# Values of a sliding-window attention kept in planes of token residues, and loaded in 16 DMAs of 1 MB instead of 128 of 128 KB

## The chip, the core and the metric

The kernel runs on one core of a Trainium2 chip. The metric is the device time of one execution in microseconds (us). The kernel before took 205.69, 203.16 and 200.42 us in three runs; the median is 203.16 us. The profile that is read here is of one execution that took 202.74 us, of which 201.0 us are the span that the profile covers; the other 1.74 us lie around it.

## What is computed

```python
x = A_x                                   # 1 x 2048 x 512, bf16
xn = _layernorm(x)
s = _A_ref(xn, A_wqkv, A_wo)              # attention
g = _silu(_B_ref(xn, B_w1, B_w2, B_w3, B_w4))
return x + s * g

# _A_ref: H = 32 heads of Dh = 16, window W = 8, dilation 2
idx = pos[:, None] - (arange(W) * 2)[None, :]      # token t looks at t, t-2, ..., t-14
logits = einsum("bhsd,bhswd->bhsw", q, kg) * scale # kg, vg: k and v gathered by idx
logits = where(idx >= 0, logits, -1e9)
o = einsum("bhsw,bhswd->bhsd", softmax(logits), vg)
return o @ wo

# _B_ref: a token-shift mixer and an MLP, both with a residual
h = _gelu(_layernorm(x) @ w1)             # quarters of h shifted by +1, -1, +2, -2 tokens
x1 = x + shifted(h) @ w2
return x1 + _gelu(_layernorm(x1) @ w3) @ w4       # w3 512 x 1376, w4 1376 x 512
```

## The kernel before

The 2048 tokens are 16 tiles of 128 tokens and four chunks of four tiles. Nothing is planned at run time: the string ORDER lists about 800 named steps, and the program issues them in that order, so each engine and each DMA queue works through its own steps in the order of that string. A name is a step and a tile (or a chunk and a part): h8 is the step h of tile 8, qk1.3 is part 3 of chunk 1. The steps that the text speaks of:

- st, rsa, rsb, rsc, xn: the first layer norm of a tile (statistics on VectorE, the power -0.5 on GpSimd, the normalized tile on VectorE for chunk 0 and on ScalarE after). tr, xe turn chunk 0 and 1 over on TensorE; tx (line 339) turns the tiles of chunks 2 and 3 over by DMA. xc2 and xc3 load the inputs of those chunks, w3.n and w4.n the MLP's weights.
- h, v, qk: the products with w1, wv and wqk, four matmuls each; he, ve, qe evict them on ScalarE. hst (line 426) turns h over by DMA. vst (line 416) stores a tile of v, 128 tokens x 1 KB, from one of three buffers to the DRAM scratch v_dram, on GpSimd's DMA queue.
- pw, lg: q times k shifted by 2u tokens on VectorE, and the sum over a head's 16 numbers on TensorE, for u = 0 to 7. mask, mx, ls, ex, to, sh, et, ae: the softmax of a chunk and its turn into the tile att. The mask of chunk 0 is seven memsets of -1e9 (line 464).
- lv (line 655): the values of one tile, loaded back from the scratch. A partition of the tile vs holds the pair (u mod 4, token mod 32); along it lie four blocks of 32 tokens and the two halves of u. Each u is a DMA of its own with 128 rows of 1 KB, so a tile takes eight DMAs in two halves (lv5.0 and lv5.1 are u = 0 to 3 and 4 to 7 of tile 5). vs has three buffers.
- pr (line 661): vs times att in place on VectorE. ws (line 670): the sum over u by eight matmuls with the 0/1 matrix sel. oe evicts the sum, oTe (line 690) turns it over by DMA, for the last three tiles on TensorE (ot). wo multiplies by wo, sg and fa multiply by the gate and add x, out stores.
- mix (line 553), xo, s3, xm, x1T (line 586): the mixer of a tile, its layer norm and its turn by DMA. w3c.n and ge: one of the eleven parts of the first MLP product of chunk c and its gelu; w4, yy, si: the second product of a tile and the gate. pl and pr_ copy a few columns of h between neighbouring chunks on GpSimd.

SyncE's queue (SP) issues all loads but two, all DMA transposes and the output stores, each waiting in turn for what it needs.

Of the kernel before, what the change touches and what calls it, by code (L numbers as in the profile page):

```python
# [9 lines left out]
ALU = mybir.AluOpType  # L10
# [7 lines left out]
xn2 rsa3 tr1 xn3 tr2 xe1 xe2 tr3 r2a0 h1 xe3 r2q0 h2 r2b0 he0 h3 v0 he2 hst0 qk0.6 ve0 st6 he1 qk0.0 vst0 w3.1  # L18
st7 qe0.6 pl0 hst1 v2 qe0.0 st4 qk0.3 ve2 st5 hst2 vst2 he3 rsa1.0 qe0.3 rsb1.0 lv0.0 v1 qk0.5 ve1 rsc1.0 r2a1
xn6 qk0.2 vst1 hst3 qe0.5 r2b1 qk0.1 xn4 xc3 qe0.2 mix1 lv0.1 qe0.1 qk0.7 xn5 xo1 xn7 qk0.4 s31 xc2 qe0.7  # L20
tr1.0 qe0.4 lv1.0 tr1.1 xe1.0 mix0 qa1 pw0.0 h4 xe1.1 lv1.1 v5 he4 xo0 qk1.2 st12 ve5 qk1.7 vst5 s30 hst4
qe1.2 st11 lg0.0 qe1.7 qk1.0 lv2.0 pl1 st8 h7 qe1.0 st10 qk1.4 w4.1 he7 st9 qk1.5 lv2.1 pw0.2 qe1.4 pr_0 h5
qe1.5 rsa2.0 st14 rsb2.0 qk1.6 he5 hst7 st15 v3 qe1.6 rsc2.0 hst5 st13 xn8 mix2 r2a2 ve3 v4 tx8 rsa3.0 xn10
r2b2 pw0.1 mix3 xn9 tx10 xo2 rsb3.0 ve4 v7 xo3 xn11 qk1.1 vst4 s32 tx9 ve7 vst3 rsc3.0 qk1.3 r2a3 qe1.1 vst7
w3.0 s33 xn15 lg0.2 r2b3 tx11 lg0.1 pw0.7 qe1.3 h6 xn12 mix4 ra30 he6 pw0.5 rb30 xn13 h8 hst6 xo4 xn14 v8 rc30
s34 he8 v6 xm2 hst8 h10 ve8 ve6 vst8 tx12 lg0.7 xm0 lg0.5 vst6 pw0.4 v10 he10 pl2 x1T0 xm3 h9 pw0.6 ve10 pr_1
tx13 h11 he9 vst10 lg0.6 he11 lg0.4 tx15 mix5 pw0.3 mix7 x1T2 pw1.0 qa2 v11 tx14 xo7 qk2.7 ve11 xo5 w3.3 qk2.1
vst11 s37 qe2.7 w3.2 v13 s35 qe2.1 hst10 xm1 qk2.3 ve13 x1T3 lg0.3 qe2.3 qk2.2 vst13 mask x1T1 qk2.4 pw1.1
qe2.2 v9 hst11 qe2.4 mx0 mix6 ve9 hst9 ls0 v12 vst9 h14 w4.2 xo6 ve12 ex0 s36 qk2.5 vst12 h12 ra31 rb31 v14
he14 to0 w4.0 lg1.0 h15 rc31 sh0 w30.7 qe2.5 he12 qk2.0 ve14 hst12 he15 pw1.2 w30.4 vst14 ge0.7 pl3 hst14 et0  # L30
qe2.0 pr_3 w30.5 ge0.4 ae0 xm5 hst15 w30.9 pr0 ge0.5 w30.1 xm4 pr_2 ge0.9 qk2.6 x1T4 ge0.1 pr1 xm7 ws0 x1T5
lg1.2 qe2.6 lg1.1 w30.10 oe0 lv3.0 pw1.5 v15 ge0.10 w30.8 pw1.3 ve15 x1T7 w30.3 vst15 ge0.8 pr2 xm6 lg1.3
lg1.5 lv3.1 ge0.3 w30.2 w30.6 ge0.2 pw1.4 x1T6 w30.0 ge0.6 pw1.7 ws2 ge0.0 oTe0 lg1.4 oe2 ws1 pw1.6 lg1.7 w42
lv4.0 pw2.4 qa3 pr3 oTe2 qk3.6 oe1 oTe1 w41 qe3.6 yy2 lv4.1 si2 ws3 yy1 lg1.6 w40 oe3 lv5.0 mx1 si1 pw2.0 oTe3
ls1 mix9 lv5.1 qk3.5 xo9 ex1 yy0 mix10 s39 mix8 lv6.0 xo10 qk3.7 qe3.5 xo8 si0 to1 qk3.4 lv6.1 w31.2 s38 qe3.7
w43 qe3.4 sh1 ge1.2 s310 qk3.1 yy3 et1 qe3.1 w31.8 ae1 si3 w31.6 pr4 w31.4 ge1.8 w31.10 pr5 wo.3 mix11 wo.2
ge1.10 w31.9 ge1.4 ge1.6 w31.7 xo11 ge1.9 wo.1 pr6 ws5 ge1.7 lg2.0 oe5 ws4 lg2.4 oe4 lv7.0 w31.3 pw2.1 wo1
ge1.3 pw2.3 wo0 lv7.1 w31.5 sg1 s311 w31.1 ge1.5 oTe5 fa1 wo2 ra32 ge1.1 sg0 rb32 lv8.0 lg2.3 sg2 lg2.1 w31.0
pw2.6 qk3.0 ge1.0 out1 rc32 pw2.5 oTe4 xm8 h13 qe3.0 pr7 w45 xm11 x1T8 he13 xm9 lv8.1 fa0 wo3 fa2 yy5 lg2.5
x1T9 sg3 si5 lg2.6 qk3.3 pw2.2 hst13 w47 pw2.7 qe3.3 xm10 x1T11 fa3 lg2.2 out3 yy7 lg2.7 out2 ws7 out0 mx2 si7  # L40
ws6 x1T10 qk3.2 oe7 oe6 ls2 w44 oTe7 qe3.2 pw3.2 ex2 oTe6 pw3.0 w46 lv9.0 yy4 to2 si4 lv9.1 mix12 yy6 w32.5
sh2 si6 mix14 lv10.0 ge2.5 w32.8 xo12 xo14 et2 ge2.8 lv10.1 w32.1 s312 ae2 w32.10 ge2.1 s314 mix15 ge2.10 pr8
w32.6 mix13 ge2.6 w32.7 xo15 xo13 wo6 ge2.7 s315 wo5 s313 w32.0 sg5 lg3.0 ra33 sg6 ge2.0 ws8 rb33 lg3.2 pr10
oe8 lv11.0 w32.2 w32.4 ge2.2 w32.9 oTe8 rc33 ge2.4 pr9 xm12 w32.3 lv11.1 ge2.9 wo7 xm14 pw3.4 wo4 ge2.3 xm13
x1T12 w411 sg7 sg4 x1T14 pw3.5 x1T13 ws10 fa5 yy11 lg3.5 oe10 lg3.4 w48 pr11 si11 out5 oTe10 xm15 pw3.7 w49
x1T15 yy8 pw3.1 si8 lg3.7 fa4 ws9 pw3.6 out4 lg3.1 oe9 w410 lv12.0 fa7 pw3.3 oTe9 yy9 lg3.6 yy10 lg3.3 si9
ws11 lv12.1 mx3 w33.0 si10 oe11 wo8 fa6 ge3.0 ls3 oTe11 wo10 sg8 w33.2 ex3 lv13.0 sg10 w33.10 fa8 fa10 w33.4
out8 ge3.2 w33.7 to3 out10 lv13.1 w33.5 sh3 ge3.7 w33.8 ge3.10 out6 w33.6 ge3.4 lv14.0 ge3.8 w33.9 ge3.5 ge3.6
et3 ge3.9 w33.1 out7 ae3 lv14.1 w33.3 pr12 ge3.1 wo11 ge3.3 wo9 sg11 ws12 sg9 w412 oe12 lv15.0 fa11 fa9 pr13
out9 w415 lv15.1 pr14 out11 w414 oTe12 yy15 yy12 si15 ws14 yy14 ws13 si12 pr15 w413 oe14 oe13 si14 ot14 yy13  # L50
wo12 oTe14 si13 ws15 sg12 ot13 oe15 wo14 fa12 oTe13 out12 ot15 sg14 wo13 oTe15 fa14 wo15.0 sg13 out14 wo15.1
sg15.0 fa13 out15.0 sg15.1 out13 out15.1
# [4 lines left out]
def kernel(  # L57
# [35 lines left out]
    NB = P // T32  # L93

# [26 lines left out]
    oTp = pool("oTp", 4)  # L121
# [5 lines left out]
    v_dram = dram.tile([PADK + S, D], BF16, name="v_dram")  # L127
# [43 lines left out]
    sel = const.tile([P, T32], BF16, name="sel")  # L171

# [4 lines left out]
    nc.gpsimd.dma_start(out=v_dram[0:PADK, :], in_=zrows[0:PADK, :])  # L177
# [82 lines left out]
    def plan_ln1(c, t, dk):  # L260
# [63 lines left out]
        def tr1(i):  # L324
            if i == 0:
                ps["tr0"] = ps_lg.tile([P, 2, 2, ND, P], BF16, name="tr0_ps", tag="lg")
            pt = ps["tr0"][:, i % 2, i // 2, :, :]
            for dt in range(ND):
                nc.tensor.transpose(pt[:, dt, :], xn_t[i][:, dt * P : (dt + 1) * P], ident[:])

        def xe1(i):
            if i == 0:
                xnT_t[0] = xnTp.tile([P, ND, CH], BF16, name="xnT", tag="xnT")
            nc.scalar.activation(xnT_t[0][:, :, i * P : (i + 1) * P], ps["tr0"][:, i % 2, i // 2, :, :], AF.Copy)  # L334
# [43 lines left out]
    def plan_qkv(c, keys):  # L378
# [36 lines left out]
        def v_s(i):  # L415
            nc.gpsimd.dma_start(out=v_dram[PADK + i * P : PADK + (i + 1) * P, :], in_=vc_t.pop(i))  # L416
# [28 lines left out]
    def plan_logits(c, t, dk):  # L445
# [16 lines left out]
        def mask():  # L462
            for u in range(W - 1):
                nc.vector.memset(lg_t[c][0:32, u, 0 : PADK - DIL * u], -1e9)
# [36 lines left out]
        def turn():  # L501
            pt = ps[f"et{c}"] = mm_tile("et_ps", (P, NB, 2, P), BF16)
            E_n = E_t.pop(c)
            for b in range(NB):
                for uh in range(2):
                    nc.tensor.transpose(  # L506
                        pt[:, b, uh, :],
                        E_n[:, b, U4 * uh : U4 * uh + U4, :].rearrange("p u t -> p (u t)"), ident[:])

        def at_e():  # L510
            at_t[c] = attp.tile([P, NB * 2, TPC, H], BF16, name="att", tag="att")
            nc.vector.tensor_copy(
                out=at_t[c].rearrange("p n j h -> p n (j h)"),
                in_=ps.pop(f"et{c}").rearrange("p b u q -> p (b u) q"))
# [131 lines left out]
    def plan_attend(i, t, tw):  # L646
        c, jj = i // TPC, i % TPC

        def load_vs(uh):
            if uh == 0:  # L650
                vs_t[i] = vsp.tile([P, NB, 2, D], BF16, name="vs", tag="vs")
            vs = vs_t[i]
            for u in range(U4 * uh, U4 * uh + U4):
                r0 = i * P + DIL * u
                nc.sync.dma_start(
                    out=vs[T32 * (u % U4) : T32 * (u % U4) + T32, :, u // U4, :],
                    in_=v_dram[r0 : r0 + P, :].rearrange("(b t) d -> t b d", t=T32))

        def prod():
            vv = vs_t[i].rearrange("p b u (dh h) -> p (b u) dh h", dh=DH, h=H)  # L660
            nc.vector.tensor_tensor(  # L661
                out=vv, in0=vv,
                in1=at_t[c][:, :, jj, :].unsqueeze(2).to_broadcast([P, NB * 2, DH, H]), op=ALU.mult)

        def gather():
            vs = vs_t.pop(i)
            pt = ps[f"o{i}"] = mm_tile("o_ps")
            for uh in range(2):
                for b in range(NB):
# [14 lines left out]
        def ot_e():  # L684
            oT_t[i] = oTp.tile([P, ND, P], BF16, name="oT", tag="oT")
            nc.scalar.activation(oT_t[i], ps.pop(f"ot{i}"), AF.Copy)

        def od():
            oT_t[i] = oTp.tile([P, ND, P], BF16, name="oT", tag="oT")
# [110 lines left out]
```

## Time and profile before

| | us | where |
|---|---|---|
| profiled execution | 202.74 | span 201.0 and 1.74 around it |
| VectorE busy | 165.6 | 82% of the span |
| ScalarE busy | 132.5 | 66% |
| GpSimd busy | 30.8 | 15% |
| products pr on VectorE | 36.3 | 16 of 2287 ns, 128x4096 bf16 |
| sums ws on TensorE | 9.4 | 128 matmuls |
| value loads lv | 128 issues of 302 / 430 / 2331 ns (least, median, most) on SP | 2.3 / 3.0 / 7.3 us from issue to landing |
| value stores vst | 16 issues of 544 ns (median) on GpSimd | 2.0 / 2.9 / 5.4 us to landing |
| turns hst, tx, x1T, oTe | 53 DMA transposes, some 1.2 us of SP each | 2.5 to 3.5 us to landing (medians) |

The page of a profile gives busy times by engine, the span in 40 slices, the DMA queues, the chain of work that ended last, the costliest groups of instructions by line, and the DMA issues. Further views answer for a stretch of time: busy times by window with the mean busy share of the 16 DMA engines and the rate, the instructions in order of time, and who waited for whom. The DMA share of a window can exceed 1 a little, since a packet's time is put to the stretch in which it began.

### The profile page before, as it was taken

What the parts mean: (1) busy time and instruction counts of PE and PEld (TensorE: products, weight loads), DVE (VectorE), ACT (ScalarE), POOL (GpSimd) and SP (SyncE); (2) the same over time, 40 slices, a digit from 0 to 9 for tenths busy, and PEclk for the clock granted to TensorE, in tenths of its full rate; (3) what the DMA queues carried; (4) which work ended last, traced back from release to release, by engine and by line L of the source; (5) the groups of instructions that cost most, each with busy time, mean ns of one, the idle gap of its engine ahead of it and who ended that gap; (6) DMA issues with size and microseconds to landing.
All of it is one profiled execution on the core that took longest, in us unless ns stands there. A gap on an engine that the chain in (4) does not pass through costs nothing.

```text
span 201.0 us, 3994 instructions
## 1 busy us (share of the span) xinstructions
PE 187.4 (93%) x1470; PEld 90.0 (45%) x1496; DVE 165.6 (82%) x265; ACT 132.5 (66%) x204; POOL 30.8 (15%) x48
## 2 busy tenths in 40 slices
PE   7599999939999999999999999999999999999991
PEld 7344544413444444454444444445444444444440
DVE  5752667993496799997999999899999999689854
ACT  3498856595837799727689639497446629953370
POOL 4015220692731411120000020000020000000000
PEclk9999999996999999999999999999999999999999
DMA  5988999999699654766985446666937567798302
GB/s 186 343 260 188 256 248 256 253 141 243 153 108 258 165 169 95 203 144 179 224 215 139 116 126 181 176 116 172 252 76 203 129 138 186 215 258 248 93 29 79
DMA packets 57908, 36.27 MB, mean 180 GB/s; under 512 B 31794, under 2 KB 56864, under 8 KB 57888
## 3 DMA queue, kind: packets, MB, share of 16 engines
q1 hardware_dynamic: 56416, 33.24, 67.8%
q0 software_dynamic: 800, 2.11, 3.2%
q10 hardware_dynamic: 672, 0.66, 1.0%
q8 instruction: 12, 0.20, 0.4%
q14 instruction: 8, 0.07, 0.2%
HBM read 24.84 MB, written 4.21 MB: 145 GB/s over the span
## 4 chain that ended last, share of the span: by engine, by line
PE 86%; DMA 4%; ACT 4%; DVE 3%; issue 1%; ACTq 0%; DVEq 0%
PE w_ps L608 19%; PE w_ps L623 19%; PE qk_ps L393 13%; PE v_ps L405 7%; PE w_ps L553 6%; PE h_ps L405 6%; PE wo_ps L715 6%; PE lg L457 4%; PE o_ps L670 4%; DMA xnT<-xn 3%; DMA x_all<-in_A_x_dram 1%; DVE stats L262 1%; PE et_ps L506 1%; ACT vct L411 1%; ACT xn L308 1%
## 5 line engine op out<-in xcount | busy, mean ns | idle before, releaser
L448 DVE TENSOR_TENSOR pw<-qT,kT 128x2048 bf16<-128x2048 bf16 x32 | 38.2, 1216 | 5.3 <-PE lg L457 5.1
L608 PE MATMUL w_ps<-x1nT,w_sb 128*128 128x512 bf16 (+1 forms) x168 | 41.1, 380 | 0.4
L623 PE MATMUL w_ps<-w_sb,h3t 128*128 128x512 bf16 (+1 forms) x171 | 39.4, 379 | 0.5 <-issue 0.3
L661 DVE TENSOR_TENSOR vs<-vs,att 128x4096 bf16<-128x4096 bf16 x16 | 36.3, 2287 | 0.2
L615 ACT ACTIVATE h3t<-w_ps 128x512 bf16<-128x512 f32 (+1 forms) x44 | 25.1, 605 | 12.9 <-PE w_ps L608 12.6
L393 PE MATMUL qk_ps<-xnT,wqk_sb 128*128 128x512 bf16 x122 | 30.4, 379 | 0.5 <-issue 0.3
L623 PEld LDWEIGHTS <-h3t 128*128 128x128 bf16 (+1 forms) x176 | 16.7, 98 | 20.7 <-issue 0.8
L608 PEld LDWEIGHTS <-w_sb 128*128 128x128 bf16 (+1 forms) x176 | 16.9, 100 | 19.1 <-DMA vs<-v_dram 0.4
L405 PEld LDWEIGHTS <-xnT 128*128 128x128 bf16 x128 | 12.6, 101 | 16.8 <-issue 2.3
L553 PE MATMUL w_ps<-w_sb,hT 128*128 128x512 bf16 x63 | 16.2, 379 | 3.6 <-DMA hT<-ht 3.6
L393 PEld LDWEIGHTS <-wqk_sb 128*128 128x128 bf16 x128 | 12.2, 98 | 14.9 <-issue 0.4
L676 ACT ACTIVATE o_sb<-o_ps 128x512 bf16<-128x512 f32 x16 | 9.5, 598 | 12.8 <-DMA oT<-o_sb 3.7
L405 PE MATMUL v_ps<-wv_sb,xnT 128*128 128x512 bf16 x62 | 17.2, 398 | 0.1
L405 PE MATMUL h_ps<-w_sb,xnT 128*128 128x512 bf16 x61 | 16.0, 393 | 1.0 <-ACT xnT L334 0.7
L632 ACT ACTIVATE g<-g 128x512 bf16<-128x512 bf16 x16 | 10.0, 629 | 10.1 <-DVE g L629 10.0
L262 DVE BATCH_NORM_STATS2 stats<-x_all 128x6 f32<-128x512 bf16 x16 | 10.8, 675 | 4.7 <-DMA x_all<-in_A_x_dram 4.7
L715 PE MATMUL wo_ps<-wo_sb,oT 128*128 128x512 bf16 x59 | 14.5, 379 | 0.2
L416 POOL DMA_DIRECT2D v_dram<-vct x16 | 9.0, 563 | 36.5 <-ACT vct L411 36.5
L420 ACT ACTIVATE ht<-h_ps,rstd 128x512 bf16<-128x512 f32 x16 | 10.9, 687 | 5.0 <-issue 2.0
L571 POOL TENSOR_TENSOR rstd<-ve,mhalf 128x4 f32<-128x4 f32 x4 | 4.3, 1067 | 58.4 <-DVE ve L566 58.4
L580 ACT ACTIVATE xn<-x,nmr,rstd 128x512 bf16<-128x512 bf16 x16 | 13.1, 819 | 0.0
L629 DVE TENSOR_TENSOR g<-w_ps,x 128x512 bf16<-128x512 f32 x16 | 10.7, 681 | 2.8 <-PE w_ps L623 2.8
(84 smaller groups left out, 234.0 us busy)
## 6 DMA issues: line engine op xcount, KB each, us to landing
vs<-v_dram SPq DMA_DIRECT2D x128, 128.0 KB, 3.0
v_dram<-vct POOLq DMA_DIRECT2D x16, 128.0 KB, 2.9
out_dram<-x_all SPq DMA_DIRECT2D x15, 128.0 KB, 2.5
x_all<-in_A_x_dram SPq DMA_DIRECT2D x3, 512.0 KB, 7.0
w_sb<-in_B_w_dram SPq DMA_DIRECT2D x4, 344.0 KB, 3.9
w_sb<-in_B_w_dram SPq DMA_DIRECT2D x2, 640.0 KB, 5.9
wqk_sb<-in_A_wqkv_dram SPq DMA_DIRECT2D x2, 512.0 KB, 6.4
w_sb<-in_B_w_dram ACTq DMA_DIRECT2D x1, 512.0 KB, 4.9
```

What stands on the lines that cost most here:

```text
L262: nc.vector.bn_stats(out=stats1[:, i, :], in_=x_all[:, i, :])
L393: nc.tensor.matmul(pt, lhsT=wqk_sb[:, dt, nt * P : (nt + 1) * P], rhs=xnT_t[c][:, dt, :], start=(dt == 0), stop=(dt == ND - 1))
L405: nc.tensor.matmul(pt, lhsT=xnT_t[c][:, dt, jj * P : (jj + 1) * P], rhs=w_sb[:, dt, :], start=(dt == 0), stop=(dt == ND - 1))
L420: nc.scalar.activation(ht_t[i], ps.pop(f"h{i}"), AF.Gelu_apprx_tanh, scale=rstd2[:, i : i + 1])
L448: nc.vector.tensor_tensor(out=pw, in0=q_t[c], in1=k_t[c][:, :, DIL * u : DIL * u + CH], op=ALU.mult)
L553: nc.tensor.matmul(pt, lhsT=hT_t[c][:, g, b0 + shift[g] : b0 + shift[g] + P], rhs=w2_sb[:, g, :], start=(g == 0), stop=(g == ND - 1))
L580: nc.scalar.activation(xn3_t[i], x1_t[i], AF.Identity, bias=nmr3[:, i : i + 1], scale=rstd3[:, i : i + 1])
L608: nc.tensor.matmul(pt[:fs, :], lhsT=w3_sb[:, dt, ft * P : ft * P + fs], rhs=x1nT_t[c][:, dt, :], start=(dt == 0), stop=(dt == ND - 1))
L615: nc.scalar.activation(h3_t[c, ft][:fs, :], ps.pop(f"w3{c}.{ft}")[:fs, :], AF.Gelu_apprx_tanh)
L623: nc.tensor.matmul(pt, lhsT=h3_t[c, ft][:fs, jj * P : (jj + 1) * P], rhs=w4_sb[:fs, ft, :], start=(ft == 0), stop=(ft == NF - 1))
L661: nc.vector.tensor_tensor(out=vv, in0=vv, in1=at_t[c][:, :, jj, :].unsqueeze(2).to_broadcast([P, NB * 2, DH, H]), op=ALU.mult)
L715: nc.tensor.matmul(pt, lhsT=oT[:, dt, :], rhs=wo_sb[:, dt, :], start=(dt == 0), stop=(dt == ND - 1))
```

## The change

The scratch becomes 64 planes of 65 rows. A token goes to plane 32 + (token mod 32), row token div 32, and a second time to plane (token mod 32), one row on, so that the row of a token shifted by 2u is found by a step of 2u planes alone. Each tile is so stored twice. A load then takes a pair of tiles and one half of u: for each partition one run of 8 rows, 8 KB. The tile vs holds such a half pair, again in three buffers. Products, sums, the turn of the softmax and the attention's output go by pairs; each instruction works on as many elements as before. The mask of chunk 0 becomes one addition of a constant tile that seven memsets on GpSimd prepare (an eighth clears it). The order of steps is a new one throughout.

```diff
+    NQ = S // T32 + 1
...
-    v_dram = dram.tile([PADK + S, D], BF16, name="v_dram")
+    v_dram = dram.tile([2 * T32, NQ, D], BF16, name="v_dram")
...
+    nc.gpsimd.memset(maskb[:], 0.0)
+    for u in range(W - 1):
+        nc.gpsimd.memset(maskb[0:T32, u, 0 : PADK - DIL * u], -1e9)
+    nc.gpsimd.dma_start(out=v_dram[T32 - PADK : T32, 0, :], in_=zrows[0:PADK, :])
...
-            pt = ps["tr0"][:, i % 2, i // 2, :, :]
+            pt = ps["tr0"][:, i % 2, 0, :, :]
...
         def v_s(i):
-            nc.gpsimd.dma_start(out=v_dram[PADK + i * P : PADK + (i + 1) * P, :], in_=vc_t.pop(i))
+            vt = vc_t.pop(i)
+            nc.gpsimd.dma_start(
+                out=v_dram[T32 : 2 * T32, i * NB : (i + 1) * NB, :].rearrange("m q d -> q m d"), in_=vt)
+            nc.gpsimd.dma_start(
+                out=v_dram[0:T32, i * NB + 1 : (i + 1) * NB + 1, :].rearrange("m q d -> q m d"), in_=vt)
...
         def mask():
-            for u in range(W - 1):
-                nc.vector.memset(lg_t[c][0:32, u, 0 : PADK - DIL * u], -1e9)
+            nc.vector.tensor_tensor(
+                out=lg_t[c][:, :, 0:PADK], in0=lg_t[c][:, :, 0:PADK], in1=maskb[:], op=ALU.add)
...
         def at_e():
-            at_t[c] = attp.tile([P, NB * 2, TPC, H], BF16, name="att", tag="att")
+            at_t[c] = attp.tile([P, 2, TPC, NB, H], BF16, name="att", tag="att")
             nc.vector.tensor_copy(
-                out=at_t[c].rearrange("p n j h -> p n (j h)"),
-                in_=ps.pop(f"et{c}").rearrange("p b u q -> p (b u) q"))
+                out=at_t[c], in_=ps.pop(f"et{c}").rearrange("p u b (j h) -> p u j b h", h=H))
...
-    def plan_attend(i, t, tw):
+    def plan_attend(p, t):
...
         def load_vs(uh):
-            if uh == 0:
-                vs_t[i] = vsp.tile([P, NB, 2, D], BF16, name="vs", tag="vs")
-            vs = vs_t[i]
-            for u in range(U4 * uh, U4 * uh + U4):
-                r0 = i * P + DIL * u
-                nc.sync.dma_start(
-                    out=vs[T32 * (u % U4) : T32 * (u % U4) + T32, :, u // U4, :],
-                    in_=v_dram[r0 : r0 + P, :].rearrange("(b t) d -> t b d", t=T32))
+            vs_t[p, uh] = vsp.tile([P, 2 * NB, D], BF16, name="vs", tag="vs")
+            m0 = T32 - PADK + DIL * U4 * uh
+            rows = v_dram[m0 : m0 + T32 + DIL * (U4 - 1), 2 * NB * p : 2 * NB * (p + 1), :]
+            src = bass.AP(
+                tensor=rows.tensor, offset=rows.offset,
+                ap=[[DIL * NQ * D, U4], [NQ * D, T32], [1, 2 * NB * D]])
+            nc.sync.dma_start(out=vs_t[p, uh].rearrange("q r d -> q (r d)"), in_=src)
...
+        def prod(uh):
+            vv = vs_t[p, uh].rearrange("q r (dh h) -> q r dh h", dh=DH, h=H)
+            at = at_t[c][:, uh, 2 * k : 2 * k + 2, :, :].rearrange("q j b h -> q (j b) h")
             nc.vector.tensor_tensor(
...
+                out=vv, in0=vv, in1=at.unsqueeze(2).to_broadcast([P, 2 * NB, DH, H]), op=ALU.mult)
+
+        def gather(a):
+            pt = ps[f"o{p}.{a}"] = mm_tile("o_ps")
             for uh in range(2):
...
+                for s in range(4):
                     nc.tensor.matmul(
+                        pt[T32 * s : T32 * s + T32, :], lhsT=sel[:], rhs=vs_t[p, uh][:, 4 * a + s, :],
+                        start=(uh == 0), stop=(uh == 1), tile_position=(0, T32 * s))
```

In the new names p is a pair of tiles: lvp.uh and prp.uh load and multiply one half of u, wsp.a, oep.a and oTep.a belong to one of its two tiles. The new order, as far as the text follows it, by engine:

```text
SP      ... hst0 hst1 hst2 xc2 hst3 xc3 lv0.0 lv0.1 hst4 lv1.0 hst7 hst6 tx8 hst5 tx9 tx10 tx11 tx12 tx13
        tx15 hst8 tx14 x1T0 x1T1 x1T2 hst10 w3.2 hst12 hst9 w3.3 w3.0 w4.2 w3.1 x1T3 wo.2 w4.0 hst11 hst14
        hst15 x1T4 x1T6 x1T5 w4.1 x1T7 lv1.1 lv2.0 oTe0.0 oTe0.1 hst13 wo.1 lv2.1 oTe1.0 lv3.0 oTe1.1 wo.3
        lv3.1 lv4.0 out2 out3 x1T8 x1T11 x1T9 oTe2.0 x1T10 oTe2.1 out0 out1 lv4.1 lv5.0 oTe3.0 oTe3.1 lv5.1
        lv6.0 oTe4.0 oTe4.1 x1T12 x1T14 x1T15 x1T13 out4 out7 lv6.1 lv7.0 out5 oTe5.0 oTe5.1 out6 out9 out8
        lv7.1 oTe6.0 oTe6.1 out11 out10 oTe7.0 ...
TensorE ... h3 v1 v0 qk0.1 v3 v2 qk0.7 qk0.6 mix0 qk0.4 mix1 tr1.0 qk0.5 qk0.0 tr1.1 h4 qk0.3 mix2 v5 h7 h6
        qk1.0 v4 qk0.2 h5 qk1.1 qk1.5 qk1.6 v7 qk1.2 mix3 v6 qk1.7 lg0.0 qk1.3 qk1.4 lg0.4 lg0.5 v8 h8 mix6
        ... h15 et0 lg1.4 w30.6 ... w30.10 ws0.1 lg1.7 lg1.3 ws0.0 ... ws3.0 lg3.4 lg3.6 mix12 w32.3 lg3.2
        w32.5 w32.0 mix13 w32.7 w32.8 w32.1 mix14 ws4.1 ws4.0 ... ws6.0 ws6.1 w412 w413 w414 w415 ws7.0 ws7.1
        wo12 ot7.0 wo13 ot7.1 wo14 wo15.0 wo15.1
```

## The prediction

> **What bounds the kernel now.** First the page's busy times and slices.
>
> ```profile
> PE 187.4 (93%) x1470; PEld 90.0 (45%) x1496; DVE 165.6 (82%) x265; ACT 132.5 (66%) x204; POOL 30.8 (15%) x48
> ...
> PE   7599999939999999999999999999999999999991
> ...
> DMA  5988999999699654766985446666937567798302
> ```
>
> TensorE is busy for 187.4 of 201.0 us; the ninth slice (40 to 45 us) is its one hole inside. Next the windows (busy us by engine, granted clock, DMA share, GB/s), to see how deep the hole is:
>
> ```profile
> 30.00:41.00 11.00, 10.82 (x80) 5.06 (x80) 9.34 (x24) 6.92 (x12) 3.86 (x4) 1.00 1.04 251
> 41.00:46.40 5.40, 1.66 (x8) 0.42 (x6) 4.60 (x13) 5.23 (x9) 5.38 (x6) 1.00 1.35 176
> 46.40:56.00 9.60, 9.40 (x93) 4.21 (x96) 4.46 (x7) 6.42 (x10) 3.88 (x6) 0.82 0.76 178
> 70.00:85.00 15.00, 14.84 (x152) 7.33 (x144) 14.63 (x15) 13.44 (x24) 2.14 (x5) 1.00 0.58 153
> 190.00:201.00 11.00, 6.57 (x46) 2.98 (x44) 6.21 (x12) 3.69 (x7) 0.00 (x0) 0.96 0.15 49
> ```
>
> Of 13.6 us of idle TensorE, 3.7 lie in the hole (and the clock is low behind it), 4.4 in the tail, 3.5 in the first 10 us; some 2 us are left for the rest. From 70 us on TensorE is full and VectorE nearly. The instructions in order of time say who made the hole:
>
> ```profile
> 33.03 1.95 SPq L655 DMA_DIRECT2D vs<-v_dram  x4
> 35.02 0.43 SPq L214 DMA_DIRECT2D w_sb<-in_B_w_dram  x1
> 35.50 1.96 SPq L655 DMA_DIRECT2D vs<-v_dram  x4
> 37.55 3.27 SPq L426 DMA_TRANSPOSE hT<-ht  x2
> 40.93 4.48 SPq L339 DMA_TRANSPOSE xnT<-xn  x3
> 45.39 0.82 PE L553 MATMUL w_ps<-w_sb,hT 128*128 128x512 bf16 x3 [3.56 <-DMA hT<-ht]
> 46.39 1.75 PE L405 MATMUL h_ps<-w_sb,xnT 128*128 128x512 bf16 x4 [0.17 <-DMA xnT<-xn]
> ```
>
> SP is busy without a break, value loads ahead of the turns, and the DMA engines are full (1.04): tx8, issued at 40.93, lands only at 46.3. From the end of h3 (12.76) to et0 (73.62) TensorE has 59 groups of four matmuls (0.863 each, from 1.73 for two in the chain of waits), nine lg of 0.315, and 0.9 of turns: 54.65 us of work in 60.86. So 6.2 us are lost here, the most that the change can win.
>
> **The change, part by part.** Small edits first. The mask: seven memsets (0.5 us in all) become one 128x112 f32 addition, between 0.15 (128x4 rows) and 0.36 (128x256 f32); I take 0.25, so 0.2 saved, hidden. The mask's eight GpSimd memsets at 0.1 each go ahead of k's padding, which is first read at 24 us: 0 (0.8 if read at once). Products: same elements, 16 x 2287 ns. ae writes in another order: 682 ns each, at worst the 1216 of a two-input product, up to 2.1 us in four, over VectorE's 35 idle us: 0. tr2 must now wait for xe0 (ended 6.6, tr2 at 8.2): 0. Stores: 16 more GpSimd issues of 0.54, 8.7 us on an engine with 170 idle; rsb2.0 is queued behind vst5's second one, but no longer behind pr_0 (a wait of 6.8 us at 35.15 before): 0, at most 0.5. With three buffers for v's copies ve2 must wait for vst1's second store: v1 leaves TensorE at 13.6, ve1 at 14.5, that store is issued at 15.5 and lands 2.9 later, 18.4, where v2 and ScalarE's queue would let ve2 start at 17.7; six PSUM tiles hide 1 us on ScalarE, without them it costs 1. SP: 128 issues of 0.43 become 16 of 0.43 to 0.58 (the rows of 128 and 512 KB DMAs), 55 us to 8, of which 10 ahead of tx8. By the new order xn8 waits only for ve4: v4 is the 20th group after h3, done at 12.76 + 20 x 0.863 + 0.9 = 30.9, ve4 at 31.7, xn8 (0.81) at 32.6. So tx8 could go out at 32.7 instead of 40.93; TensorE wants it at 12.76 + 32 groups + 3 lg + 0.9 = 42.2.
>
> What decides is **how a 1 MB load runs**, which no row shows. All loads of before begin, in the DRAM pattern, with a dimension of 32, 96 or 128; the new one begins with U4 = 4. If a DMA is divided by rows or bytes, all sixteen engines carry it; if by the first dimension, four do. For the price per engine:
>
> ```profile
> 5.00:9.00 4.00, 2.65 (x24) 1.73 (x23) 3.69 (x15) 1.72 (x5) 0.00 (x0) 1.00 1.01 337
> 61.00:67.00 6.00, 6.00 (x43) 2.68 (x42) 4.51 (x11) 3.58 (x7) 1.08 (x2) 1.00 0.90 231
> 139.00:143.00 4.00, 3.95 (x25) 2.18 (x25) 3.91 (x8) 2.17 (x4) 0.00 (x0) 1.00 0.92 249
> ```
>
> At full share, input loads with 1 KB rows move 337/1.01 = 334 GB/s, value loads alone 249/0.92 = 270, turns 231/0.90 = 257. 1.049 MB are 3.1 us on sixteen engines; on four 12.5 by the first and 15.5 by the second. Turns (packets under 512 B) to 1 KB rows, the rate rises with the packet, and 8 KB packets should gain more: I take 11, with 9.6 to 12.5 as the likely range and 15.5 as the far end.
>
> I take four engines. The rows fit both divisions, but the one DMA whose count isn't a multiple of 16, the 14 zero rows on GpSimd, took 5.6 us for 14 KB where stores of 128 KB take 2.9; weak, since it ran in the crowd of the start, but on that side. The Trainium skill (DMA: Bandwidth & Descriptors, "Why a DMA increments its semaphore by 16 and not by 1") says that the number of engines is the largest up to 16 that divides the slowest dimension of both patterns, which here is 4, and that the sync queue takes the lowest-numbered ones; no run here has such a load yet. By that page's 27 GiB/s per engine a load would take 9.0 us and the sum below would be 241.
>
> The sum on four engines, always the same four: lv0.0 can start at about 21 (vst0's second store: ve0 ends at 15.8, GpSimd is at it behind vst1 and pl0, issued by 17.5, plus 2.9, and SP's own wait). In front of tx8 on these engines lie three loads, 33 us, four turns of 0.5 (128 KB at 257) and some 3 us of stores: 59, landing 61.5 with the least latency of 2.3. So v8 starts at 61.5, not 42.2; et0 follows after 26 groups and 6 lg (24.3) at 85.8, and the end of ws0.0 after 11.8 at 97.6. There vs buffers come free and the other 13 loads start. A pair needs two loads, 22 us, but after its own last load lands only product 2.3, sums 1 and waits 0.5 before the next is issued, so the engines never run dry: 13 x 11 = 143, with 23 turns (11.5) and 12 stores of output (5) between them, last landing at 97.6 + 159.5 + 2.3 = 259.4. Product 2.6, then two sums and the tail (8.6 from ws15 to the end before, so 9): span 271, with 1.74 outside **273 us**. Of 9.6 or 12.5 per load 16 times the difference: 251 to 297; at 15.5, 345. This is against the profiled 202.74; the median lies 0.4 above, which I leave.
>
> **Rivals.** (1) *Sixteen engines.* A load lands in about 2.3 + 2.8 = 5.1 us. Bytes ahead of tx8 are those of before (1 MB of weights out, 1 MB of second stores in), but issued before 28 us, so it lands by 37, 5 us early. The hole goes whole: 202.74 - 6.2 = 196.5 us, faster. For it: SP's and xn8's relief is real in either case. Against: needs the other division. The Trainium skill (same page, Bandwidth) advises 1 MiB per DMA or more and measured 6.15 us for one; by that the sum would be 196.8.
> (2) *Sixteen engines, but the ring of half pairs is late.* The second half of a pair can only be issued when the pair before has been summed. By TensorE's new order the work between two pairs less product and waits (2.8) leaves a load 9.8 us (pairs 1, 2), 5.9 (pair 4: nine groups, three lg), 6.7 (pair 7: four w4 of 2.38); others have over 10. At 9 us to landing this costs 3.1 + 2.3 = 5.4: 202 us, no change. For it: 512 KB loads took 4.9 to 9.7 in the crowd of the start. Against: later the share is 0.6.
> (3) The same ring above 10.7 us to landing costs over 10.6 and ends above 207.2, slower, though on sixteen engines: 208 to 230.
>
> **How the numbers follow.** Two per cent, about what a measurement of this kernel can tell from no change, is 199.1 to 207.2. Four engines 0.72 (the shape of the pattern, and the 14 rows; what keeps it lower is that the rows fit the other division too), rival 1 0.14, rival 2 0.08, rival 3 0.06. Faster 0.14, same 0.08, slower 0.78. Predicted 273, own range 250 to 297. To leave out no more than 2 in 10 the range goes from 203, through rival 3 and part of 2, to 305.
>
> **What would show it.** Right: value loads of 11 to 14 us to landing alone and over 20 in pairs, the DMA share near 0.3 to 0.4 while they run alone, at some 90 to 105 GB/s; a hole of some 20 us before v8; VectorE waiting for vs at the second half of each pair. Wrong: landing near 5 us and over 250 GB/s, no hole at 42 us. If the engines are four but SP is held while it issues, turns come later still and 273 is too low; if pairs leave gaps between loads, too.

## The result and the profile after

| | before | after |
|---|---|---|
| median, us | 203.27 | 363.02 |
| profiled execution, span, us | 202.74, 201.0 | 362.27, 360.2 |
| TensorE busy, us | 187.4 (93%) | 218.0 (61%) |
| DMA queue of SP (q1), MB and share of 16 engines | 33.24, 67.8% | 33.37, 84.2% |
| issues of value loads | 128 | 16 |
| stores of v, median to landing, us | 2.9 | 7.2 |

The kernel after is slower by a factor of 1.793 (95% interval 1.769 to 1.817). Where a median further down takes in executions at a disturbed clock, the ratio beside it leaves them out; for one kernel (e14) only one of four executions was undisturbed, and its time is named.

First the page of the kernel after, busy times and slices (a slice is now 9 us):

```profile
PE 218.0 (61%) x1492; PEld 96.3 (27%) x1492; DVE 166.2 (46%) x259; ACT 133.8 (37%) x204; POOL 38.0 (11%) x72
...
PE   6969600039789979595040968892677539408815
...
PEclk9989955558989989899555796998589667957978
...
DMA  8889529239989999992933229499239259959931
```

VectorE works as long as before (166.2 us against 165.6). TensorE's work itself has become longer (218.0): the granted clock falls to 0.5 in and behind the long stretches of idleness (the fives of PEclk stand at and behind the zeros of PE), and four matmuls that take 0.86 us at the full clock take 1.87 there (the row at 77.84 below). The first three zeros of PE, 45 to 72 us, are the old hole at 41 to 46 us, grown. The windows (busy us of PE, PEld, DVE, ACT, POOL, then granted clock, DMA share, GB/s) show what the DMA engines did there:

```profile
30.00:41.00 11.00, 11.00 (x52) 5.00 (x51) 9.12 (x27) 5.97 (x9) 2.68 (x4) 1.00 2.73 110
42.90:53.00 10.10, 0.00 (x0) 0.00 (x0) 0.00 (x0) 0.00 (x0) 0.00 (x0) 0.63 0.25 95
53.00:63.00 10.00, 0.00 (x0) 0.00 (x0) 0.00 (x0) 0.00 (x0) 0.00 (x0) 0.50 2.20 85
63.00:72.00 9.00, 0.00 (x0) 0.00 (x0) 0.00 (x0) 0.00 (x0) 0.00 (x0) 0.50 0.26 64
```

From 42.9 to 53 us nothing runs but value loads, at a share of 0.25: four of sixteen engines, at 95 GB/s together. So 1.049 MB take 11.0 us. The shares over 2 in the first and third row are no work: a packet's whole time is put to the stretch in which it began, so these are packets that began there and were held for tens of microseconds. By queue and size, the packets of the first row that were held for over 3 us are eleven of GpSimd's queue, which are stores of v (258 us together), and six of 256 B, a turn's (156 us); in the third row 273 of 303 us are a turn's. So stores and turns are both held while the loads run. What this does to the turns shows in SP's instructions in order of time (start, us, then the operation):

```profile
26.28 1.25 SPq L664 DMA_DIRECT2D vs<-v_dram  x2
31.68 11.02 SPq L435 DMA_TRANSPOSE hT<-ht  x1
42.88 1.37 SPq L664 DMA_DIRECT2D vs<-v_dram  x1
44.34 27.74 SPq L435 DMA_TRANSPOSE hT<-ht  x2
72.19 1.21 SPq L344 DMA_TRANSPOSE xnT<-xn  x1
...
296.38 1.28 SPq L664 DMA_DIRECT2D vs<-v_dram  x2
...
298.38 21.41 SPq L699 DMA_TRANSPOSE oT<-o_sb  x2
```

A turn that took SP some 1.2 us before takes it 11 to 14 us in the mean of these rows, where it is issued behind loads; all 54 turns together hold SP for 210 us, the 53 before for 69. SP stands still in it, so tx8 (the xnT at 72.19) goes out 31 us later than at 40.93 before, and not some 8 us sooner. The chain of waits (start, us, what) has the same turns and the loads in turn:

```profile
31.68 45.31 DMA hT<-ht
77.84 1.87 PE qk_ps L398 x4
...
131.59 16.27 DMA vs<-v_dram
...
181.88 31.40 DMA vs<-v_dram
...
298.38 26.81 DMA oT<-o_sb
...
330.53 16.91 DMA vs<-v_dram
```

By engine this chain is 61% DMA and 14% TensorE. One more thing is seen only in the packets. Between 227.2 and 237.5 us:

```profile
DMA packets 2848, 0.88 MB, mean 85 GB/s; under 512 B 2592, under 2 KB 2848, under 8 KB 2848
```

All packets are under 2 KB, so none is a value load's, whose rows are 8 KB: the bottleneck of the stage stands empty for 10 us.

### The profile page after: what moved, and what is told of

It reads as the page before. It is cut to its first block, busy times and chain, and to the rows that moved or that the text cites. A ratio compares the mean times of both kernels' runs of the same rounds, so it can differ in the third digit from the quotient of the medians.

```text
span 360.2 us, 3881 instructions
## 1 busy us (share of the span) xinstructions
PE 218.0 (61%) x1492; PEld 96.3 (27%) x1492; DVE 166.2 (46%) x259; ACT 133.8 (37%) x204; POOL 38.0 (11%) x72
## 3 DMA queue, kind: packets, MB, share of 16 engines
q1 hardware_dynamic: 40640, 33.37, 84.2%
## 4 chain that ended last, share of the span: by engine, by line
DMA 61%; PE 14%; DVE 9%; SPq 6%; ACT 5%; issue 4%; POOL 0%; ACTq 0%; DVEq 0%; POOLq 0%
DMA vs<-v_dram 24%; DMA hT<-ht 13%; DMA oT<-o_sb 12%; DMA x1nT<-xn 6%; SPq L699 5%; DMA x_all<-in_A_x_dram 4%; PE w_ps L616 3%; PE wo_ps L740 2%; PE qk_ps L398 2%; DMA xnT<-xn 2%; DVE vs L669 2%; PE o_ps L676 1%; ACT xn L588 1%; DVE g L745 1%; PE w_ps L561 1%
## 5 line engine op out<-in xcount | busy, mean ns | idle before, releaser
L669 DVE TENSOR_TENSOR vs<-vs,att 128x4096 bf16<-128x4096 bf16 x16 | 36.4, 2288 | 87.7 <-DMA vs<-v_dram 87.7
L616 PE MATMUL w_ps<-x1nT,w_sb 128*128 128x512 bf16 (+1 forms) x176 | 47.6, 421 | 14.8 <-DVE x L567 13.5
L398 PE MATMUL qk_ps<-xnT,wqk_sb 128*128 128x512 bf16 x128 | 33.4, 403 | 35.7 <-ACT ht L429 35.7
L631 PE MATMUL w_ps<-w_sb,h3t 128*128 128x512 bf16 (+1 forms) x176 | 43.2, 404 | 0.0
L676 PE MATMUL o_ps<-vs,sel 128*32 128x512 bf16 x128 | 12.9, 488 | 45.5 <-DVE vs L669 43.3
L740 PE MATMUL wo_ps<-wo_sb,oT 128*128 128x512 bf16 x60 | 22.0, 509 | 27.4 <-DMA oT<-o_sb 21.9
L616 PEld LDWEIGHTS <-w_sb 128*128 128x128 bf16 (+1 forms) x176 | 18.8, 110 | 39.4 <-issue 23.9
L561 PE MATMUL w_ps<-w_sb,hT 128*128 128x512 bf16 x64 | 19.5, 430 | 6.6 <-DMA hT<-ht 3.5
L745 DVE TENSOR_TENSOR g<-wo_ps,g 128x512 bf16<-128x512 f32 x15 | 10.2, 687 | 19.3 <-PE wo_ps L740 11.3
L740 PEld LDWEIGHTS <-oT 128*128 128x128 bf16 x60 | 6.6, 119 | 39.5 <-DMA oT<-o_sb 23.3
L676 PEld LDWEIGHTS <-sel 128*32 128x32 bf16 x128 | 3.7, 106 | 50.1 <-DMA vs<-v_dram 33.3
```

What stands on the lines that cost most here:

```text
L398: nc.tensor.matmul(pt, lhsT=wqk_sb[:, dt, nt * P : (nt + 1) * P], rhs=xnT_t[c][:, dt, :], start=(dt == 0), stop=(dt == ND - 1))
L561: nc.tensor.matmul(pt, lhsT=hT_t[c][:, g, b0 + shift[g] : b0 + shift[g] + P], rhs=w2_sb[:, g, :], start=(g == 0), stop=(g == ND - 1))
L616: nc.tensor.matmul(pt[:fs, :], lhsT=w3_sb[:, dt, ft * P : ft * P + fs], rhs=x1nT_t[c][:, dt, :], start=(dt == 0), stop=(dt == ND - 1))
L631: nc.tensor.matmul(pt, lhsT=h3_t[c, ft][:fs, jj * P : (jj + 1) * P], rhs=w4_sb[:fs, ft, :], start=(ft == 0), stop=(ft == NF - 1))
L669: nc.vector.tensor_tensor(out=vv, in0=vv, in1=at.unsqueeze(2).to_broadcast([P, 2 * NB, DH, H]), op=ALU.mult)
L676: nc.tensor.matmul(pt[T32 * s : T32 * s + T32, :], lhsT=sel[:], rhs=vs_t[p, uh][:, 4 * a + s, :], start=(uh == 0), stop=(uh == 1), tile_po ...
```

## The experiments

**Loads on sixteen engines.** In e1 the load's DRAM pattern is turned so that it begins with 32. For that the partitions of vs are ordered (token mod 32, u mod 4), sel too, and the shares E_n are written in that order, by two products per chunk.

```diff
-                ap=[[DIL * NQ * D, U4], [NQ * D, T32], [1, 2 * NB * D]])
+                ap=[[NQ * D, T32], [DIL * NQ * D, U4], [1, 2 * NB * D]])
```

> The changed kernel with the load's DRAM pattern turned round: the 32 token residues first, the four shifts second, still one DMA of 1 MB with 8 KB runs. Partition order of att and of sel follows (the product of the shares is written in two halves per chunk). Theory A, the first dimension sets the number of DMA engines (4 in the change, 16 here): a load lands in 5 to 7 us, the hole before v8 is gone, 195 to 202 us. Theory B, the loads are slow because of their size, their 8 KB runs or the 65 KB step between planes: it stays above 300 us.

Measured: 214.50 us (214.32 to 215.97; before 203.30 beside it), loads landing in 6.8 us at the median (5.4 to 9.8). In the list of DMA issues of e1 (operation, number, KB, median us to landing):

```profile
vs<-v_dram SPq DMA_DIRECT2D x16, 1024.0 KB, 6.8
```

The one turned pattern takes away 148.5 of the 160 us. But 195 to 202 was expected and 11 us are left.

In e2 the pattern stays in its order but each load is cut into four by its first dimension, 32 partitions x 8 KB each.

```diff
+            for w in range(U4):
+                m = m0 + DIL * w
                 nc.sync.dma_start(
-                    out=vs_t[p, uh].rearrange("q r d -> q (r d)"), in_=src)
+                    out=vs_t[p, uh][T32 * w : T32 * w + T32, :, :],
+                    in_=v_dram[m : m + T32, 2 * NB * p : 2 * NB * (p + 1), :])
```

> The changed kernel with four DMAs for each half pair, one for each shift: 32 partitions, 8 KB runs, 64 loads of 256 KB. First dimension 32. Theory A: as e1, 195 to 203 us, with SP's issues at 64 x 0.43 = 28 us instead of 7. Theory B with size as the cause: faster than the change too, but then e1 stays slow; with runs or the step between planes as the cause: above 300 us, like e1.

Measured: 221.94 us (220.00 to 222.96). Without e1's second product for the shares it also loses the large part and keeps a rest, 18.6 us over before.

**What the rest is.** The stores, too, have a DRAM pattern that begins with a dimension of 4 (q, the token div 32 within the tile). In e3 the kernel before gets one such store more per tile, to a scratch that nobody reads.

```diff
             nc.gpsimd.dma_start(out=v_dram[PADK + i * P : PADK + (i + 1) * P, :], in_=vt)
+            nc.gpsimd.dma_start(
+                out=v_pl[T32 : 2 * T32, i * NB : (i + 1) * NB, :].rearrange("m q d -> q m d"), in_=vt)
```

> The kernel before, unchanged but for one more DMA per tile of v: it is also stored to a second scratch in planes, with a DRAM pattern that begins with a dimension of 4 as in the change; nobody reads that scratch. Theory S (the stores by planes run on four engines and hold up the turns, and that is most of what the change still costs once its loads are on sixteen engines, 214.5 against 203.3): 205 to 211 us, and the turns of the early stage land in over 4 us at the median instead of 2.5 to 3.3. Theory L (the large early loads hold up the turns, the stores are harmless): 202 to 205, landing times of the turns unchanged.

Measured: 207.87 us against 202.02, ratio 1.025 (1.015 to 1.036). The list of DMA issues of e3:

```profile
hT<-ht SPq DMA_TRANSPOSE x16, 5.2
...
xnT<-xn SPq DMA_TRANSPOSE x8, 5.6
```

The turns of h land in 5.2 us at the median instead of 3.2, those of xn in 5.6 instead of 3.5. One more store of 128 KB per tile costs some 5 us by the ratio, although GpSimd is busy for only 37.6 of 205 us: theory S.

e9 is e1 with the same number of stores and the same bytes, but with a pattern that begins with 32. The tokens of a tile so land in other places of the scratch: its loads bring back the values of other tokens, and its time tells what the same work costs, not how to repair the change.

```diff
-                out=v_dram[T32 : 2 * T32, i * NB : (i + 1) * NB, :].rearrange("m q d -> q m d"), in_=vt)
+                out=v_dram[T32 : 2 * T32, i * NB : (i + 1) * NB, :], in_=vt)
...
-                out=v_dram[0:T32, i * NB + 1 : (i + 1) * NB + 1, :].rearrange("m q d -> q m d"), in_=vt)
+                out=v_dram[0:T32, i * NB + 1 : (i + 1) * NB + 1, :], in_=vt)
```

> The variant with loads on sixteen engines (214.5 us), in which the two stores of a tile write the same bytes with a DRAM pattern that begins with 32 (plane, then row) instead of 4; still two issues of GpSimd per tile. The tokens of a tile so go to other places of the scratch, and the values that are loaded back are not those of the reference; the work is the same. Theory S (stores on four engines hold up the turns, worth what one more such store cost before, 5.9 us, or more): 202 to 209, stores landing near 3 us, turns near 3. Theory O (the order of the steps and what hangs on it costs the 11 us, not the stores): 212 to 216.

Measured: 201.41 us (200.88 to 203.41) against 201.53, ratio 1.0015 (0.998 to 1.005). The 11 us were the stores, all of them. The lists of DMA issues show how they worked. Of e1:

```profile
hT<-ht SPq DMA_TRANSPOSE x16, 5.4
...
xnT<-xn SPq DMA_TRANSPOSE x8, 6.6
```

and of e9:

```profile
v_dram<-vct POOLq DMA_DIRECT2D x32, 128.0 KB, 3.9
...
hT<-ht SPq DMA_TRANSPOSE x16, 4.1
...
xnT<-xn SPq DMA_TRANSPOSE x8, 3.0
```

With the turned pattern the stores land in 3.9 us (7.2 after), and the turns of xn are back at 3.0 us. While any 4 KB packet of a store is in flight (those held for over 1 us left out), it is 8.5 at once in the mean in e9 and 4.5 in e1, which fits stores on few engines in e1. But e9 changes a second thing: the four rows of a plane now lie side by side, 4 KB instead of 1 KB. Windows of e9 for the old hole and the stretch behind it:

```profile
41.00:46.40 5.40, 5.35 (x69) 2.48 (x68) 4.11 (x7) 5.29 (x10) 3.27 (x5) 1.00 0.77 167
46.00:60.00 14.00, 13.75 (x136) 6.44 (x137) 12.99 (x22) 9.24 (x15) 5.66 (x14) 1.00 0.82 173
```

The hole is gone: TensorE has 5.35 of 5.40 us where it had 1.66.

In e6, on e1 too, the stores are spread in another way, with rows of 1 KB apart as in the change: each is divided by q into four DMAs, eight per tile.

```diff
+            for q in range(NB):
+                rows = vt[T32 * q : T32 * q + T32, :]
+                nc.gpsimd.dma_start(out=v_dram[T32 : 2 * T32, i * NB + q, :], in_=rows)
+                nc.gpsimd.dma_start(out=v_dram[0:T32, i * NB + q + 1, :], in_=rows)
```

> The variant with loads on sixteen engines (214.5 us), in which each store of a tile is divided into four DMAs of 32 partitions x 1 KB, whose patterns begin with 32; GpSimd issues eight small stores per tile instead of two. Theory S: 200 to 208, the turns back near 3 us to landing, DMA share between 46 and 60 us clearly below 1. Theory L: 212 to 217. What speaks against S even if it is right about the engines: eight issues of some 0.7 us are 5.5 us of GpSimd per tile, and the first load waits for the stores.

Measured: 223.81 us. The stores land in 2.8 us and the turns in 3.8 (h) and 3.6 (xn) instead of 5.4 and 6.6 in e1, so the hold-up shrinks with the pattern although the rows are 1 KB. But now the stores' issue is the bound; the page's chain by engine of e6 (in e1 GpSimd had 0% of it):

```profile
DVE 34%; PE 32%; POOL 21%; DMA 5%; issue 4%; ACT 2%; DVEq 0%; ACTq 0%
```

128 issues of 0.5 us on GpSimd (64 us), with the powers of the layer norms queued behind them. So e6's time doesn't speak against S; it tests another price.

Two other explanations of the 11 us were tried. e8 is e1 with its first three loads issued some 30 us later in the order:

```diff
-r2a1 mix0 qe0.6 lv0.0 rsc1.0 xn5 qk0.4 r2b1 lv0.1 xo0 ...
+r2a1 mix0 qe0.6 rsc1.0 xn5 qk0.4 r2b1 xo0 ...
...
-... xm3 lg0.2 hst10 mix7 ...
+... xm3 lg0.2 lv0.0 lv0.1 hst10 mix7 ...
...
-xo7 qa2 hst12 ...
+xo7 qa2 lv1.0 hst12 ...
```

> The variant with loads on sixteen engines (214.5 us), in which the first three loads (pair 0 both halves, pair 1 first half) are issued behind the turns of the third chunk's inputs and of the mixer's first tiles, some 30 us later. Theory L: the hold-ups of the turns before 60 us go, 203 to 209. Theory S: those hold-ups stay, 212 to 217; were the loads to land too late for the first products, more.

Measured: 220.55 us, slower than e1, and the turns land no sooner (of h in 7.5 us at the median, of xn in 6.3), so the early loads aren't what holds the turns up there: theory L falls.

e10 is e1 with the exponentials written in the turn's order, so that the shares are one product again; e11 is e9 with that product.

```diff
-            Ec_t[c] = smp.tile([P, W, P], BF16, name="E_c", tag="E_c")
-            nc.scalar.activation(Ec_t[c], lg_t.pop(c), AF.Exp)
+            Ec_t[c] = smp.tile([P, 2, P, U4], BF16, name="E_c", tag="E_c")
+            nc.scalar.activation(
+                Ec_t[c].rearrange("p s t u -> p s u t"),
+                lg_t.pop(c).rearrange("p (s u) t -> p s u t", u=U4), AF.Exp)
...
+            E_n = E_t[c] = ep.tile([P, 2, P, U4], BF16, name="E_n", tag="E_n")
+            nc.vector.tensor_tensor(
+                out=E_n, in0=Ec_t.pop(c),
+                in1=rinv_b.unsqueeze(1).unsqueeze(3).to_broadcast([P, 2, P, U4]), op=ALU.mult)
```

> The variant with loads on sixteen engines (214.5 us), in which the exponentials are written in the order that the turn wants, so that the shares of a chunk are one product of VectorE again and not two of 1.23 us. Theory D (VectorE is full from 100 us on, so each us saved there counts): 209 to 212. Theory S: the early stalls set the time, 213 to 216.

> The stores whose pattern begins with 32 (tokens permuted within a tile, values other than the reference's) and the single product for the shares, both on the variant with loads on sixteen engines (214.5 us). Theory S with D: 198 to 206, about the time of the kernel before or less. Theory O: 208 to 214.

Measured: e10 218.52 us, ratio to before 1.078 (1.066 to 1.090); what VectorE saves does not show in the time, and theory D falls. e11: 201.92 us, as e9.

**Where the other 90 us of the forecast's error lie.** In e4 the 14 turns of the attention's output go over TensorE instead of the DMA queue; loads and stores are those of the change.

```diff
         def od(a):
-            nc.sync.dma_start_transpose(out=oT_at(a), in_=o_t.pop((p, a)))
+            ot(a)
+            ot_e(a)
```

> The changed kernel, loads as they are, but the attention's output is turned over on TensorE and evicted by ScalarE for all pairs, not by DMA for the first seven: 14 fewer DMA transposes on SP. Theory F, the turns only queue in line with the loads on the four engines: 14 x 0.5 us less, 350 to 358 us. Theory H, a turn and a 1 MB load in flight hold each other and SP: the chain's 12.2% of waiting for oT and SP's 4.8% (61 us) mostly go, 295 to 325 us.

Measured, in one execution: 321.58 us. Fourteen turns of 128 KB cost 41 us in this kernel, some 3 us each, although TensorE now does them.

In e5 the loads are issued by GpSimd's queue instead of SP's.

```diff
-            nc.sync.dma_start(out=vs_t[p, uh].rearrange("q r d -> q (r d)"), in_=src)
+            nc.gpsimd.dma_start(out=vs_t[p, uh].rearrange("q r d -> q (r d)"), in_=src)
```

> The changed kernel with the 16 loads on GpSimd's queue instead of SP's. The pattern is the same, so four engines for a load. If these are always the same four and the price is theirs alone (theory F): the loads cost what they did and the time stays at 330 to 363 us. If SP's queue behind the loads is the larger part (theory H), or if GpSimd's loads go to changing engines so that two run side by side: 210 to 270 us. A load alone should take 11 to 14 us to landing in any case.

Measured, in one execution: 390.01 us; neither theory's numbers. A load lands 33.8 us (median) after its issue. The list of waits (who, for whom: us in all, times, longest) of e5:

```profile
DVE vs L669 <- DMA vs<-v_dram: 141.6, 7, 25.6
POOL vs L664 <- PE o_ps L676: 124.4, 5, 38.0
```

VectorE waits longer for the loads than in the change (141.6 us against 87.7), and GpSimd, whose queue also holds the stores and the powers, waits for free buffers. The queue is no way out. Packets of 8 KB of several loads are in flight at once there (eight for 122 us, twelve for 22; in the change four for 190 of 226), yet in no 10 us do they move more than 105 GB/s, and in the change 106: loads side by side were together no faster than one. On which engines they ran, no view shows.

e12 is the change with e9's stores (pattern beginning with 32), e13 has e4's turns in addition.

> The change itself, loads on four engines (363.0 us), with the stores whose pattern begins with 32 (the tokens of a tile go to other places, so the values are not the reference's; same bytes, same issues). The forecast missed by 90 us: 34 before the first sums (131.6 us instead of 97.6), 54 in the stage of the 13 loads (216 us instead of 162), 1 at the end. Theory S4 (stores on the same four engines are a good part of the early 34): 333 to 352, first sums end at 100 to 118 us. Theory T (turns and 1 MB loads hold each other, with or without stores): 354 to 365, first sums stay at 125 or later. The late stage has no stores of v and should stay at 16 to 17 us per load under both.

> The same, and the turns of the attention's output on TensorE as well (321.6 us when that was done alone). If the two act in different stages and add up: S4 290 to 312, T 313 to 323. The sum of the forecast, 273, would hold only if nothing but loads of 11 us filled the late stage: 13 x 11 + 12 = 155 us from the first sums to the last landing.

Measured: e12 343.81 us, ratio 1.698 (1.684 to 1.711), e13 307.72, ratio 1.517 (1.505 to 1.529). The stores are worth 19 us here and the output's turns 36 more (41 in e4): they nearly add up, with S4's numbers for both. The first sums of e12 end at 114.5 us (in its profiled execution, which took 351.5).

e14 and e16 are e12 and e13 with the first three loads issued later: two behind the turns tx8 to tx15, hst8 and x1T0 to x1T2, one behind hst15.

```diff
-r2a1 mix0 qe0.6 lv0.0 rsc1.0 xn5 qk0.4 r2b1 lv0.1 xo0 xn4 mix1 ...
+r2a1 mix0 qe0.6 rsc1.0 xn5 qk0.4 r2b1 xo0 xn4 mix1 ...
...
-vst11 ve10 x1T1 h10 s34 ve9 pr_1 vst10 x1T2 h12 s35 he10 vst9 lg0.6 xm3 lg0.2 hst10 ...
+vst11 ve10 x1T1 h10 s34 ve9 pr_1 vst10 x1T2 h12 s35 he10 vst9 lg0.6 xm3 lg0.2 lv0.0 lv0.1 hst10 ...
...
-ae0 w30.6 xm4 hst15 pw1.5 vst13 xm6 ...
+ae0 w30.6 xm4 hst15 lv1.0 pw1.5 vst13 xm6 ...
```

> The change with its loads on four engines and the permuted stores (343.8 us; values not the reference's), and now the first three loads issued later: both halves of pair 0 behind the turns of the inputs of the third chunk, the first half of pair 1 behind the last turn of h of the fourth. Open is what the rest of the early loss is: first sums at 114.5 us where the forecast had 97.6. Theory H (turns that are queued with and between the 1 MB loads are held for far longer than the loads' own time): TensorE stays busy between 40 and 70 us, the first sums come at 88 to 102, the whole takes 318 to 334. Theory Q (four engines are simply busy with the loads' bytes, whenever those start): the loads start 30 us later and the end moves with them or stays, 340 to 360.

> The same with the turns of the attention's output on TensorE as well (307.7 us before this step). Theory H: 283 to 298. Theory Q: 304 to 320. If H holds here, taking turns and loads apart brings the sum of the forecast (273) back to within some 20 us, and what is then left is loads that are not issued back to back.

Measured: e14 357.09 us (its undisturbed execution 349.4), e16 310.06. Nothing is gained: theory Q's numbers. Yet the turns did go free where the loads were taken away, and were held where the loads now are. SP's instructions of e14:

```profile
36.77 10.08 SPq L344 DMA_TRANSPOSE xnT<-xn  x6
...
53.70 1.34 SPq L664 DMA_DIRECT2D vs<-v_dram  x2
55.14 10.76 SPq L435 DMA_TRANSPOSE hT<-ht  x1
...
67.24 11.11 SPq L435 DMA_TRANSPOSE hT<-ht  x2
```

and its windows:

```profile
40.00:50.00 10.00, 9.89 (x118) 4.63 (x119) 8.21 (x13) 8.32 (x14) 4.17 (x8) 1.00 0.77 168
...
70.00:80.00 10.00, 0.00 (x0) 0.00 (x0) 0.00 (x0) 0.00 (x0) 0.00 (x0) 0.59 0.25 98
```

The hole has moved from 42 to 70 us. With loads that keep four engines busy for 22 us, some turn stood behind them in both places.

**Anything besides the two patterns?** f1 has the change's order, pairs and half-pair buffers, but the scratch and the single store of before; a half pair is loaded in four DMAs of 256 KB, whose pattern begins with 32.

```diff
+            for w in range(U4):
+                r0 = 2 * p * P + DIL * (U4 * uh + w)
+                nc.sync.dma_start(
+                    out=vs_t[p, uh][T32 * w : T32 * w + T32, :, :],
+                    in_=v_dram[r0 : r0 + 2 * P, :].rearrange("(r t) d -> t r d", t=T32))
```

> The order, the pairs and the half-pair buffers of the change, but with the scratch of the kernel before: one store per tile, no planes. A half pair is loaded in four DMAs, one for each shift, of 32 partitions x 8 rows of 1 KB (256 KB each, 64 in all instead of 128 or 16), whose pattern begins with 32; the shares stay one product. Theory P (all that the change loses hangs on the two patterns that begin with 4; its order and its fewer issues are as good as the order before): 196 to 203, the hole of TensorE at 41 to 46 us gone. Theory K (the new order or the half-pair ring costs by itself, hidden so far): 204 to 215, VectorE waiting for vs in the late stage.

Measured: 207.82 us, ratio 1.035 (1.026 to 1.043): theory K. With 1 KB rows the half pairs land in 6.4 us and VectorE waits 6.2 us for vs in three places; in e9, with 8 KB rows in DMAs of 1 MB, it waits 0.4. The order and the ring do ask something of the loads, and e9's loads give it; whether f1's shorter rows or its four issues per half pair are what it lacks wasn't taken apart. No kernel that was run is faster than before beyond the interval.

## Why the prediction was right in kind and wrong in size

Slower, by loads that four engines carry, was the forecast, at 273 us with 250 to 297 as its own range; measured were 363.0. Its parts one by one:

- **Four engines, 11 us per load: right for loads alone.** The 11 was a choice between rows of other transfers. Measured were a share of 0.25, 95 GB/s, 11.0 us (the row at 42.9 us), and four packets of 8 KB in flight for 190 of the 226 us in which any are (in e1 most often sixteen); and turned to 32 the load lands in 6.8 us and the time falls by 148.5 us (e1). The rule that the Trainium skill gives (DMA: Bandwidth & Descriptors, "Why a DMA increments its semaphore by 16 and not by 1"), as many engines as the largest number up to 16 that divides the slowest dimension, is what the loads did here, and the stores fit it. The 9.0 us per load that the prediction estimated from that page were too low by 2: 95 GB/s are 24 per engine.
- **The first sums, 97.6 us: 131.6.** This is the term that failed: "In front of tx8 on these engines lie three loads, 33 us, four turns of 0.5 (128 KB at 257) and some 3 us of stores". Two prices in it are wrong (and 59 and 2.3 are 61.3, not 61.5, which changes nothing).
  - The stores, put at some 3 us here and at "0, at most 0.5" for their issues, have a pattern that begins with 4 as well, and packets of 16 B among theirs (3072 in the trace of after, none in before); with a pattern of 32 the sums come at 114.5 (e12), so some 17 of the 34.0 us are theirs, as far as an execution of 351.5 us speaks for a kernel of 343.8.
  - A turn behind loads isn't half a microsecond of bytes: it ends when the loads around it have landed, and SP stands in it. TensorE went idle at 42, as forecast, but waiting for hst4, issued at 31.68 and landed at 77.0, one of the four turns that were priced at 0.5. Of its 512 packets of 256 B, 383 had begun by 33.6 us and the other 129 began between 54 and 59.4, when the two loads ahead of it came to their end (the second landed at 59.6). The trace has 16 completion signals for it: four came at 60.0, and the other twelve only at 76.7 to 77.0, just behind the landing of the load that was issued after it at 42.88 (76.6). In e12, too, the load issued behind it lands at 68.9, hst4 at 69.2 and then tx8 at 70.3. That tx8 lands 8.8 us after the forecast's 61.5 is some half of the other 16.9; the remaining 8 lie between there and the sums, where turns of the same kind follow, and were not taken apart.
- **"So the engines never run dry: 13 x 11 = 143, with 23 turns (11.5) and 12 stores of output (5) between them": wrong twice.** From the issue at 131.6 to the last landing at 347.4 it is 215.8 us, not 161.8. By the start and length of the trace's packets of 8 KB the engines carry loads for 181 us of this, 13.9 per load, and stand without one for 33 (2 us pass before the first packet), in three gaps of 12, 7 and 10 us (the one at 227 to 237 is shown above) and small ones. With the output's turns off the queue (e13) it is 12.0 per load and 19 us of gaps, 176.1 in all (119.0 to 295.1). So with the output's turns beside them the loads are slower by some 2 us each, and SP comes late for the next pair. That turns are held where the loads are, e14 shows; why a turn landed only behind a load that was issued after it, no run here settles.
- **The end, 11.6 us from the last landing: 12.8.** Right. The three differences, 34.0, 54.0 and 1.2, are the 89.2 us by which the span exceeds 271.
- **What would show it wrong: named, and not priced.** "If the engines are four but SP is held while it issues, turns come later still and 273 is too low; if pairs leave gaps between loads, too." Both came. The rows for the first were at hand: before, too, SP was in DMA transposes for 3.27 us (two) and 4.48 (three) when the engines were full, where two take 2.4 and three 3.6.
- **Rival 1, sixteen engines, 196.5 us: not what sixteen engines give.** With loads alone on sixteen it is 214.5, with stores too 201.4. The hole is won (3.7 us of TensorE between 41 and 46.4), but between 60 and 180 us TensorE is idle for 4.4 us in e9 and 1.3 before, so most of it goes again. The second product for the shares isn't why (e11). Why, is open.

Turning the two patterns one after the other accounts for the whole: 363.0, loads turned 214.5, stores turned too 201.4, before 201.5 beside it.

## What to carry to other kernels

Read the first dimension of each DMA pattern on the DRAM side, for stores as for loads, before counting issues: 16 issues instead of 128 and rows of 8 KB instead of 1 KB cost 160 us here, because both patterns begin with 4. Price what shares engines with a slow transfer by that transfer's landing and not by its own bytes, on whichever queue it is issued; a turn of 0.5 us behind 22 us of loads was a turn of 22 and more here. And a ring of transfers that is the bound runs dry where its issuer has anything else to wait for, so add the gaps to the sum.

## What was not expected of the hardware

- A DMA transpose issued by SP next to loads on four engines holds SP itself for 11 to 14 us in the mean of a row (21.41 us for two, 27.74 for two), where it takes 1.2 alone. One landed only just behind a load that was issued after it (77.0 behind 76.6 us; in e12, 69.2 behind 68.9).
- Sixteen stores of 128 KB whose pattern begins with 4, issued from another queue, lengthen the turns of SP's queue from 3.5 to 5.6 us to landing (xn in e3), and with them the kernel by some 5 us.
- The same 1 MB load on GpSimd's queue takes 33.8 us to land at the median (e5), though eight or more of the loads' 8 KB packets are in flight for 159 of the 234 us in which any are; they move no more than 105 GB/s in any 10 us.
